# Splitting the first weight pieces of a 2:4-sparse linear layer more finely: 160, 160 and 192 columns in place of 256 and 256

## The chip, the cores and the metric

The kernel runs on one core of a Trainium2 chip. The metric is device time in microseconds (us) of one execution. Three timed executions of the kernel before gave 233.89, 233.45 and 233.73; their median is 233.73. Engines are named as in the profile: PE is TensorE (matmuls; PEld its weight loads), DVE is VectorE, ACT is ScalarE, POOL is GpSimd, and SP is the engine that here does nothing but issue DMA transfers. ACT issues transfers too.

## The reference

```python
def setup_inputs():
    B, S, D = 16, 512, 1024
    return {"x": normal(B, S, D) * 0.05, "w": normal(D, D) * 0.05, "b": normal(D) * 0.05}   # all bf16

def reference(x, w, b):
    N, M = 2, 4
    wg = w.reshape(D // M, M, D)
    mag = jnp.abs(wg)
    order = jnp.argsort(mag, 1)
    thr = jnp.take_along_axis(mag, order[:, M - N:M - N + 1, :], 1)
    mask = mag >= thr
    wp = (wg * mask).reshape(D, D)
    return jnp.einsum("bsd,df->bsf", x, wp) + b
```

In every group of four neighbouring rows of w the two entries of largest magnitude are kept in each column, and the others are set to zero. Then 8192 rows of x (64 tiles of 128) are multiplied with the 1024 x 1024 result and the bias is added.

## The kernel before, in words

The output is made in tiles of 128 rows of x by 512 columns of w (a half of the columns, h). K, 1024 long, is 8 steps of 128. A matmul of 128 x 128 weights (x) and up to 512 moving columns (w) adds into one of eight PSUM banks.

w comes in with its group of four along a free dimension (`wv`, line 60: `g p m f`, where g is the K half, m the place in the group of four). So the four candidates of a group lie side by side in one partition, and VectorE finds the mask with elementwise operations. It does this by pieces (line 61): columns 0:256, 256:512, 512:768 and 768:1024 of K half 0, then two pieces of 512 columns of K half 1. `abs_piece` (line 107, token `A.i`) makes the magnitudes, on VectorE or, for pieces 2 and 3, on ScalarE. `prep_piece` (line 122, token `P.i`) makes `hi` and `lo` (pairwise maximum and minimum), `t1`, `t2`, the threshold `thr`, the mask (line 142) and the product with w in place (line 144). For pieces 0 and 1 mask and product are made in two halves, places 0 and 1 of the group first, so that matmuls can begin with them.

The first eight tiles of x (T = 8) are treated apart, because the weights are not there yet. Their K half 0 is loaded as it lies (`load_x`, line 76), transposed on PE (`transpose_half`, line 156, token `T.t`, four 128 x 128 transposes with a stride of four), and copied from PSUM to SBUF by ScalarE (`copy_half`, line 163, token `C.t`). `mm_part` (line 170, tokens `M.i.t` and `N.i.t.m...`) multiplies tile t with piece i, for all four places m or for those named. While PE has nothing to do it runs dummy matmuls on zeros (`warm`, line 102: `W` is 512 columns, `w` 128).

Their partial sums go through `to_stage` (ScalarE, token `V`), are added to those of K half 1 (`add_stage`, `O`) and to the bias (`add_bias`, `B`). Six more tiles (`X`, `Y`) fill the time until the weights stand in natural order: `unpack` (line 149, token `U`) moves w by SBUF-to-SBUF transfers into `wp_nat`. All other x comes by transposing loads (`D`, `G`, `L`) and is multiplied in the long last loop (line 338; the last tile in `last_tile`), 50 of the 64 tiles.

The order of the instructions on every engine is written out by hand: `K` keeps the program order, the loads stand in lines 83 to 90, and all else in the string `FRONT` (line 256), which is read token by token (line 269). Each engine runs its own instructions in this order, so what is named later in `FRONT` waits behind what is named earlier on the same engine. SP's loads are one queue, ACT's two loads (line 84 and 86) another.

Of the kernel before, what the change touches and what calls it, by code (L numbers as in the profile page):

```python
# [10 lines left out]
def kernel(  # L11
# [7 lines left out]
    nc = tc.nc  # L19
    P = 128  # L20
    bf16 = mybir.dt.bfloat16
# [6 lines left out]
    B, S, D = x.shape  # L28
# [10 lines left out]
    T, F = 8, 6  # L39
# [5 lines left out]
    mags_pool = ctx.enter_context(tc.tile_pool(name="mags", bufs=3))  # L45
# [7 lines left out]
    def next_bank():  # L53
# [4 lines left out]


    wv = w.rearrange("(g p m) f -> p g m f", g=2, m=4)  # L60
    pieces = [(0, 0, 256), (0, 256, 512), (0, 512, 768), (0, 768, 1024),
              (1, 0, 512), (1, 512, 1024)]
    w_gh = {(g, h): const.tile([P, 4, FH], bf16, name=f"w_{g}_{h}") for g in range(2) for h in range(2)}

    def w_of(i):
        g, c0, c1 = pieces[i]
        return w_gh[(g, c0 // FH)][:, :, c0 % FH:c0 % FH + c1 - c0]

    def load_w(g, c0, c1, eng=nc.sync, m0=0, m1=4):
        dst = w_gh[(g, c0 // FH)][:, m0:m1, c0 % FH:c0 % FH + c1 - c0]  # L70
        K(eng.dma_start(dst, wv[:, g, m0:m1, c0:c1]))  # L71
# [4 lines left out]
    def load_x(ta, tb, eng=nc.sync):  # L76
        xt = const.tile([P, tb - ta, KH], bf16, name=f"xh_{ta}")
        src = xf[ta * P:tb * P, 0:KH].rearrange("(t p) c -> p t c", p=P)
        K(eng.dma_start(xt[:], src))  # L79
        for t in range(ta, tb):  # L80
            xh[t] = xt[:, t - ta, :]

    load_w(0, 0, 256, nc.sync, 0, 2)
    load_w(0, 0, 256, nc.scalar, 2, 4)
    load_x(0, 2)
    load_x(2, 4, nc.scalar)
    load_x(4, 6)
    load_w(0, 256, 512)
    load_x(6, 8)
    load_w(0, 512, 1024)  # L90
    bias_sb = const.tile([P, Dout], bf16, name="bias_sb")

# [9 lines left out]
    def warm(n):  # L102
        K(nc.tensor.matmul(bank[7][:, :n], lhsT=zeros[:, :P], rhs=zeros[:, :n], start=True, stop=True))  # L103
# [3 lines left out]
    def abs_piece(i, on_act):  # L107
        g, c0, c1 = pieces[i]
        n = c1 - c0
        if n <= 256:  # L110
            mag = mags_pool.tile([P, 4, n], bf16, name="mag")[:]
        else:
            mag = mag2_pool.tile([P, 4, n], bf16, name="mag2")[:]
        if on_act:
            K(nc.scalar.activation(mag, w_of(i), Act.Abs))
        else:
            for ms in (slice(0, 2), slice(2, 4)) if i == 0 else (slice(0, 4),):
                K(nc.vector.tensor_single_scalar(  # L118
                    mag[:, ms].bitcast(u16), w_of(i)[:, ms].bitcast(u16), 0x7FFF, op=Alu.bitwise_and))
        mags[i] = mag  # L120

    def prep_piece(i):
        g, c0, c1 = pieces[i]
        n = c1 - c0
        mag = mags.pop(i)
        magv = mag.rearrange("p (a j) f -> p a j f", j=2)
        hi = tmp.tile([P, 2, FH], bf16, name="hi")[:, :, :n]
        lo = tmp.tile([P, 2, FH], bf16, name="lo")[:, :, :n]
        K(nc.vector.tensor_tensor(hi, magv[:, :, 0, :], magv[:, :, 1, :], op=Alu.max))
        K(nc.vector.tensor_tensor(lo, magv[:, :, 0, :], magv[:, :, 1, :], op=Alu.min))  # L130
        t1 = tmp.tile([P, FH], bf16, name="t1")[:, :n]
        t2 = tmp.tile([P, FH], bf16, name="t2")[:, :n]
        K(nc.vector.tensor_tensor(t1, hi[:, 0, :], hi[:, 1, :], op=Alu.min))
        K(nc.vector.tensor_tensor(t2, lo[:, 0, :], lo[:, 1, :], op=Alu.max))
        thr = tmp.tile([P, FH], bf16, name="thr")[:, :n]
        K(nc.vector.tensor_tensor(thr, t1, t2, op=Alu.max))
        mask = tmp.tile([P, 4, FH], bf16, name="mask")[:, :, :n]

        halves = (slice(0, 2), slice(2, 4)) if i < 2 else (slice(0, 4),)
        for ms in halves:  # L140
            tb = thr[:, None, :].to_broadcast([P, ms.stop - ms.start, n])
            K(nc.vector.tensor_tensor(mask[:, ms], mag[:, ms], tb, op=Alu.is_ge))  # L142
        for ms in halves:
            K(nc.vector.tensor_tensor(w_of(i)[:, ms], w_of(i)[:, ms], mask[:, ms], op=Alu.mult))  # L144
# [11 lines left out]
    def transpose_half(t):  # L156
        own[(0, t)] = next_bank()
        xv = xh[t].rearrange("p (q m) -> p m q", m=4)
        dst = bank[own[(0, t)]][:].bitcast(bf16)[:, :4 * P].rearrange("p (m q) -> p m q", m=4)
        for m in range(4):  # L160
            K(nc.tensor.transpose(dst[:, m, :], xv[:, m, :], ident[:]))  # L161

    def copy_half(t):
        xt = const.tile([P, 4, P], bf16, name=f"xT_{t}")
        src = bank[own[(0, t)]][:].bitcast(bf16)[:, :4 * P].rearrange("p (m q) -> p m q", m=4)
        K(nc.scalar.copy(xt[:], src))  # L166
        xT[t] = xt


    def mm_part(q, t, c0, c1, ms=range(4)):  # L170
        g, h = divmod(q, 2)
        if c0 == 0 and (q > 0 or t >= T) and 0 in ms:
            own[(q, t)] = next_bank()
        dst = bank[own[(q, t)]][:, c0:c1]
        for m in ms:
            if t >= T:
                lhs, rhs = xN[t][:, 4 * g + m, :], wp_nat[h][:, 4 * g + m, c0:c1]
            elif g == 0:
                lhs, rhs = xT[t][:, m, :], w_gh[(0, h)][:, m, c0:c1]
            else:  # L180
                lhs, rhs = xg1[:, m, t * P:(t + 1) * P], wp_nat[h][:, 4 + m, c0:c1]
            K(nc.tensor.matmul(dst, lhsT=lhs, rhs=rhs, start=c0 == 0 and m == 0, stop=c1 == FH and m == 3))  # L182
# [54 lines left out]
    def issue_batch(t0, nb):  # L237
# [16 lines left out]


    FRONT = """
        I.1.0.512 D.0 A.0 P.0 W W W W W W W W w w T.0 T.1 C.0 T.2 T.3 C.1 w T.4 T.5 C.2 N.0.0.0 N.0.0.1 N.0.1.0
        N.0.1.1 N.0.0.2 N.0.0.3 N.0.1.2 N.0.1.3 A.1 C.3 P.1 U.0.0.0.512 I.1.512.1024 G C.4 M.0.2 C.5 M.0.3 T.6 T.7
        C.6 M.0.4 C.7 A.2 M.0.5 M.0.6 P.2 M.0.7 M.1.0 A.3 M.1.1 M.1.2 M.1.3 V.0.0 M.1.4 V.0.1 M.1.5 V.0.2 M.1.6
        V.0.3 M.1.7 V.0.4 P.3 M.2.0 V.0.5 M.2.1 V.0.6 M.2.2 V.0.7 M.2.3 M.2.4 M.2.5 M.2.6 A.4 P.4 U.1.0.0.512 D.1  # L260
        M.2.7 M.3.0 M.3.1 V.1.0 M.3.2 V.1.1 M.3.3 V.1.2 M.3.4 V.1.3 M.3.5 V.1.4 M.3.6 V.1.5 M.3.7 V.1.6 X.0.8 V.1.7
        X.0.9 V.0.8 X.0.10 V.0.9 X.0.11 V.0.10 X.0.12 V.0.11 X.0.13 V.0.12 V.0.13 A.5 P.5 U.1.1.0.512 U.0.1.0.512 Q
        L.0 L.1 N.4.0.0 N.4.1.0 N.4.2.0 N.4.3.0 N.4.0.1 N.4.1.1 N.4.2.1 N.4.3.1 N.4.0.2 N.4.1.2 N.4.2.2 N.4.3.2
        N.4.0.3 N.4.1.3 N.4.2.3 N.4.3.3 M.4.4 O.0.0 M.4.5 O.0.1 M.4.6 O.0.2 M.4.7 O.0.3 X.2.8 O.0.4 X.2.9 O.0.5
        X.2.10 O.0.6 X.2.11 O.0.7 X.2.12 O.0.8 X.2.13 O.0.9 N.5.0.0 N.5.1.0 N.5.0.1 N.5.1.1 N.5.0.2 N.5.1.2 N.5.0.3
        N.5.1.3 O.0.10 O.0.11 O.0.12 O.0.13 M.5.2 O.1.0 M.5.3 O.1.1 M.5.4 O.1.2 M.5.5 O.1.3 M.5.6 O.1.4 M.5.7 O.1.5
        O.1.6 O.1.7 Y.8 B.0.8 Y.9 B.0.9 Y.10 B.0.10 Y.11 B.0.11 Y.12 B.0.12 Y.13 B.0.13
    """
    for tok in FRONT.split():
        k, *n = tok.split(".")  # L270
        n = [int(c) for c in n]
        if k in "MN":
            g, c0, c1 = pieces[n[0]]
            h = c0 // FH
            mm_part(2 * g + h, n[1], c0 - h * FH, c1 - h * FH, n[2:] or range(4))
        elif k in "Ww":
            warm(FH if k == "W" else P)
        elif k == "A":
            abs_piece(n[0], 2 <= n[0] < 4)
        elif k == "P":  # L280
            prep_piece(n[0])
        elif k == "T":
            transpose_half(n[0])
        elif k == "C":
            copy_half(n[0])
        elif k == "Z":
            mm_part(n[0], n[1], 0, FH, n[2:])
        elif k == "I":
            load_w(*n)
        elif k == "D":  # L290
            load_fill(*n)
        elif k == "G":
            K(nc.sync.dma_start_transpose(out=xg1[:], in_=xf[0:T * P, KH:D]))
        elif k == "Q":
            for f in (slice(0, FH), slice(FH, Dout)):
                K(nc.sync.dma_start(bias_sb[:, f], b[f].partition_broadcast(P)))
        elif k == "X":
            mm_part(n[0], n[1], 0, FH)
        elif k == "V":
            to_stage(*n)  # L300
        elif k == "O":
            add_stage(*n)
        elif k == "B":
            add_bias(*n)
        elif k == "U":
            unpack(*n)
        elif k == "Y":
            bk = next_bank()
            mm_nat(n[0], 1, bk)
            evac_dve(n[0], 1, bk)  # L310
        elif k == "L":
            issue_batch(*batches[n[0]])
# [60 lines left out]
```

## Time and profile before

| | us |
|---|---|
| timed, median of 3 (233.45 to 233.89) | 233.73 |
| profiled execution: span from first to last instruction | 231.5 |
| timed median less the span | 2.2 |
| PE busy in the span | 226.3 (98%) |
| DVE busy | 119.9 (52%) |
| ACT busy | 18.8 (8%) |

The page gives the profiled execution's span and no other time of it; the timed median is of other executions of the same program, and what lies around the span is their difference.

PE's busy share over the 40 slices of the span:

```profile
PE   7999999999999999999999999999999999999995
DVE  4899887867987424424424423423433433433433
ACT  3977500000000000000000000000000000000000
```

Each digit is a slice of 5.8 us, in tenths. PE is full from the second slice on; DVE is nearly full in the first ten and half idle later; ACT works in the first five slices only. Matmul records show starts exactly and ends by a model, so rates are read from start to start. A few records are missing.

### The profile page before, as it was taken

The page shows a single profiled execution, that of the slowest core. Times are in us where ns is not written, and L with a number is a line of the kernel's source. Part 1 is how long each engine was busy: PE and PEld are TensorE (multiplying, and loading weights), DVE is VectorE, ACT ScalarE, POOL GpSimd, SP SyncE. Part 2 cuts the span into 40 slices and gives each one's busy share as a digit, 9 for nine tenths or more (in the row PEclk, how much of TensorE's full clock was granted, in tenths as well). Part 3 has the DMA queues.
Part 4 walks back from the last instruction along what each step waited for, and adds up shares of the span by engine and source line. Part 5 has one row for each costly group of instructions (what it writes and reads, how often), then busy time and mean ns, then how long its engine had stood idle before and what let it go on. Part 6 is the DMA issues. An engine that isn't in the chain of part 4 may idle for free.

```text
span 231.5 us, 2724 instructions
## 1 busy us (share of the span) xinstructions
PE 226.3 (98%) x1128; PEld 110.6 (48%) x1147; DVE 119.9 (52%) x204; ACT 18.8 (8%) x34; POOL 0.7 (0%) x6
## 2 busy tenths in 40 slices
PE   7999999999999999999999999999999999999995
PEld 3887444444444444444444444444444444444443
DVE  4899887867987424424424423423433433433433
ACT  3977500000000000000000000000000000000000
POOL 1000000000000000000000000000000000000000
DMA  6999889999847221995239822696129991122222
GB/s 194 319 200 242 190 178 178 253 246 296 295 181 272 91 83 34 239 201 172 93 75 238 230 93 91 120 258 197 63 91 197 188 249 46 47 91 91 91 93 91
DMA packets 76972, 38.19 MB, mean 165 GB/s; under 512 B 62752, under 2 KB 68896, under 8 KB 76960
## 3 DMA queue, kind: packets, MB, share of 16 engines
q1 hardware_dynamic: 67696, 20.91, 45.2%
q10 hardware_dynamic: 9264, 17.11, 20.4%
q8 instruction: 9, 0.15, 0.3%
q14 instruction: 3, 0.02, 0.0%
HBM read 3.41 MB, written 16.78 MB: 87 GB/s over the span
## 4 chain that ended last, share of the span: by engine, by line
PE 96%; DMA 2%; issue 1%; SPq 0%; DVE 0%
PE bank L338 73%; PE bank L182 16%; PE bank L234 6%; DMA xh<-in_x_dram 2%; PE bank L161 0%; SPq L79 0%; SPq L71 0%; DVE o_last L323 0%
## 5 line engine op out<-in xcount | busy, mean ns | idle before, releaser
L338 PE MATMUL bank<-wp_nat,xTb 128*128 128x512 bf16 x737 | 161.7, 379 | 0.8
L219 DVE TENSOR_TENSOR o_pair<-bank,bias_sb 128x512 bf16<-128x512 f32 x104 | 67.3, 686 | 99.6 <-PE bank L338 94.2
L338 PEld LDWEIGHTS <-xTb 128*128 128x128 bf16 x752 | 73.6, 98 | 88.7
L210 DVE TENSOR_TENSOR stage<-bank,stage 128x512 f32<-128x512 f32 x22 | 14.4, 686 | 3.9 <-PE bank L182 3.8
L182 PE MATMUL bank<-w,xT 128*128 128x256 bf16 x128 | 14.3, 273 | 0.0
L214 DVE TENSOR_TENSOR o_pair<-stage,bias_sb 128x512 bf16<-128x512 f32 x22 | 14.0, 682 | 0.0
L182 PE MATMUL bank<-wp_nat,xg 128*128 128x512 bf16 x62 | 13.9, 379 | 0.1
L182 PEld LDWEIGHTS <-xT 128*128 128x128 bf16 x128 | 12.5, 98 | 1.4
L206 ACT COPY stage<-bank 128x512 f32<-128x512 f32 x22 | 11.4, 618 | 3.9 <-PE bank L182 3.9
L182 PE MATMUL bank<-wp_nat,xfill 128*128 128x512 bf16 x47 | 10.6, 379 | 0.1
L234 PE MATMUL bank<-wp_nat,xfill 128*128 128x512 bf16 x47 | 10.5, 379 | 0.1
L182 PEld LDWEIGHTS <-xg 128*128 128x128 bf16 x64 | 6.3, 98 | 7.6
L234 PEld LDWEIGHTS <-xfill 128*128 128x128 bf16 x48 | 4.7, 98 | 5.7
L182 PEld LDWEIGHTS <-xfill 128*128 128x128 bf16 x48 | 4.7, 98 | 5.5
L338 PE MATMUL bank<-wp_nat,xTs 128*128 128x512 bf16 x32 | 7.1, 379 | 0.0
L142 DVE TENSOR_TENSOR mask<-mag,thr 128x512 bf16<-128x512 bf16 (+2 forms) x8 | 5.4, 690 | 0.2
L144 DVE TENSOR_TENSOR w<-w,mask 128x512 bf16<-128x512 bf16 (+2 forms) x8 | 5.3, 688 | 0.1
L103 PE MATMUL bank<-zeros 128*128 128x512 bf16 (+1 forms) x11 | 4.0, 533 | 1.2 <-DVE zeros L96 1.2
L338 PEld LDWEIGHTS <-xTs 128*128 128x128 bf16 x32 | 3.1, 98 | 3.8
L166 ACT COPY xT<-bank 128x512 bf16<-128x512 bf16 x8 | 4.1, 607 | 2.7 <-PE bank L161 2.7
L118 DVE TENSOR_SCALAR mag<-w 128x512 uint16<-128x512 uint16 (+2 forms) x5 | 2.3, 477 | 2.7 <-DMA w<-in_w_dram 2.7
L234 PE MATMUL bank<-wp_nat,xTb 128*128 128x128 bf16 (+2 forms) x32 | 3.7, 272 | 0.0
(20 smaller groups left out, 26.9 us busy)
## 6 DMA issues: line engine op xcount, KB each, us to landing
out_dram<-o_pair ACTq DMA_DIRECT2D x31, 512.0 KB, 2.8
wp_nat<-w SPq DMA_DIRECT2D x16, 128.0 KB, 2.8
w<-in_w_dram SPq DMA_DIRECT2D x3, 512.0 KB, 6.0
xh<-in_x_dram SPq DMA_DIRECT2D x3, 256.0 KB, 4.5
xh<-in_x_dram ACTq DMA_DIRECT2D x1, 256.0 KB, 4.0
w<-in_w_dram SPq DMA_DIRECT2D x1, 256.0 KB, 5.1
bias_sb<-in_b_dram SPq DMA_DIRECT2D x2, 128.0 KB, 3.7
out_dram<-o_pair ACTq DMA_DIRECT2D x1, 256.0 KB, 2.0
```

What stands on the lines that cost most here:

```text
L103: K(nc.tensor.matmul(bank[7][:, :n], lhsT=zeros[:, :P], rhs=zeros[:, :n], start=True, stop=True))
L118: K(nc.vector.tensor_single_scalar(mag[:, ms].bitcast(u16), w_of(i)[:, ms].bitcast(u16), 0x7FFF, op=Alu.bitwise_and))
L142: K(nc.vector.tensor_tensor(mask[:, ms], mag[:, ms], tb, op=Alu.is_ge))
L144: K(nc.vector.tensor_tensor(w_of(i)[:, ms], w_of(i)[:, ms], mask[:, ms], op=Alu.mult))
L166: K(nc.scalar.copy(xt[:], src))
L182: K(nc.tensor.matmul(dst, lhsT=lhs, rhs=rhs, start=c0 == 0 and m == 0, stop=c1 == FH and m == 3))
L206: K(nc.scalar.copy(stage[(h, t)][:], bank[own[(h, t)]][:]))
L210: K(nc.vector.tensor_tensor(st, bank[own[(2 + h, t)]][:], st, op=Alu.add))
L214: K(nc.vector.tensor_tensor(get_o(t)[:, f], stage.pop((h, t))[:], bias_sb[:, f], op=Alu.add))
L219: K(nc.vector.tensor_tensor(get_o(t)[:, f], bank[bk][:], bias_sb[:, f], op=Alu.add))
L234: K(nc.tensor.matmul(bank[bk][:, :c1 - c0], lhsT=xN[t][:, kt, :], rhs=wp_nat[h][:, kt, c0:c1], start=kt == 0, stop=kt == KT - 1))
L338: K(nc.tensor.matmul(bank[bks[h]][:], lhsT=xN[t][:, kt, :], rhs=wp_nat[h][:, kt, :], start=kt == 0, stop=kt == KT - 1))
```

## The change

The two pieces of 256 columns become three of 160, 160 and 192. The first load brings columns 0:320 (half by SP, half by ACT), and the later one 320:512. The first x load, of two tiles by SP, becomes two of one tile each, one by SP and one by ACT; tiles 2 and 3 move from ACT to SP, tiles 4 and 5 from SP to ACT; and tiles 6 and 7 go ahead of the second weight load. The magnitudes of piece 1 are made by ScalarE and of pieces 0 and 2 by VectorE. The first three pieces have mask and product in halves. `FRONT` is rewritten: four `w` dummies in place of two before T.0, transposes and matmuls of the first pieces interleaved otherwise. All later pieces have a number one higher, with the same order among them.

```diff
-    pieces = [(0, 0, 256), (0, 256, 512), (0, 512, 768), (0, 768, 1024),
+    pieces = [(0, 0, 160), (0, 160, 320), (0, 320, 512), (0, 512, 768), (0, 768, 1024),
               (1, 0, 512), (1, 512, 1024)]
...
-    load_w(0, 0, 256, nc.sync, 0, 2)
-    load_w(0, 0, 256, nc.scalar, 2, 4)
-    load_x(0, 2)
-    load_x(2, 4, nc.scalar)
-    load_x(4, 6)
-    load_w(0, 256, 512)
+    load_w(0, 0, 320, nc.sync, 0, 2)
+    load_w(0, 0, 320, nc.scalar, 2, 4)
+    load_x(0, 1)
+    load_x(1, 2, nc.scalar)
+    load_x(2, 4)
+    load_x(4, 6, nc.scalar)
     load_x(6, 8)
+    load_w(0, 320, 512)
     load_w(0, 512, 1024)
...
-            mag = mags_pool.tile([P, 4, n], bf16, name="mag")[:]
+            mag = mags_pool.tile([P, 4, 256], bf16, name="mag")[:, :, :n]
...
-        halves = (slice(0, 2), slice(2, 4)) if i < 2 else (slice(0, 4),)
+        halves = (slice(0, 2), slice(2, 4)) if i < 3 else (slice(0, 4),)
...
-        I.1.0.512 D.0 A.0 P.0 W W W W W W W W w w T.0 T.1 C.0 T.2 T.3 C.1 w T.4 T.5 C.2 N.0.0.0 N.0.0.1 N.0.1.0
-        N.0.1.1 N.0.0.2 N.0.0.3 N.0.1.2 N.0.1.3 A.1 C.3 P.1 U.0.0.0.512 I.1.512.1024 G C.4 M.0.2 C.5 M.0.3 T.6 T.7
-        C.6 M.0.4 C.7 A.2 M.0.5 M.0.6 P.2 M.0.7 M.1.0 A.3 M.1.1 M.1.2 M.1.3 V.0.0 M.1.4 V.0.1 M.1.5 V.0.2 M.1.6
...
+        I.1.0.512 D.0 A.0 A.1 P.0 W W W W W W W W w w w w T.0 T.1 C.0 T.2 T.3 w C.1 N.0.0.0.1 C.2 P.1
+        N.0.0.2.3 T.4 N.0.1.0.1 C.3 T.5 N.0.2.0.1 N.0.1.2.3 C.4 T.6 N.0.3.0.1 N.0.2.2.3 C.5 T.7 N.0.4.0.1
+        N.0.3.2.3 C.6 N.0.4.2.3 A.2 M.0.5 N.1.0.0.1 C.7 P.2 U.0.0.0.512 I.1.512.1024 G N.1.0.2.3 M.0.6
+        N.1.1.0.1 N.0.7.0.1 A.3 N.0.7.2.3 N.1.1.2.3 M.1.2 M.1.3 N.1.4.0.1 A.4 N.1.4.2.3 M.1.5 M.1.6 P.3
+        M.1.7 M.2.0 M.2.1 V.0.0 M.2.2 N.2.3.0.1 V.0.1 N.2.3.2.3 M.2.4 V.0.2 M.2.5 N.2.6.0.1 V.0.3 N.2.6.2.3
...
-            abs_piece(n[0], 2 <= n[0] < 4)
+            abs_piece(n[0], n[0] in (1, 3, 4))
```

More of the change, by code (lines that the diff above doesn't have):

```diff
@@ L256 @@
     FRONT = """
-        I.1.0.512 D.0 A.0 P.0 W W W W W W W W w w T.0 T.1 C.0 T.2 T.3 C.1 w T.4 T.5 C.2 N.0.0.0 N.0.0.1 N.0.1.0
-        N.0.1.1 N.0.0.2 N.0.0.3 N.0.1.2 N.0.1.3 A.1 C.3 P.1 U.0.0.0.512 I.1.512.1024 G C.4 M.0.2 C.5 M.0.3 T.6 T.7
-        C.6 M.0.4 C.7 A.2 M.0.5 M.0.6 P.2 M.0.7 M.1.0 A.3 M.1.1 M.1.2 M.1.3 V.0.0 M.1.4 V.0.1 M.1.5 V.0.2 M.1.6
-        V.0.3 M.1.7 V.0.4 P.3 M.2.0 V.0.5 M.2.1 V.0.6 M.2.2 V.0.7 M.2.3 M.2.4 M.2.5 M.2.6 A.4 P.4 U.1.0.0.512 D.1
-        M.2.7 M.3.0 M.3.1 V.1.0 M.3.2 V.1.1 M.3.3 V.1.2 M.3.4 V.1.3 M.3.5 V.1.4 M.3.6 V.1.5 M.3.7 V.1.6 X.0.8 V.1.7
@@ L262 @@
[L262 to L266, printed above, removed]
@@ L267 @@
-        O.1.6 O.1.7 Y.8 B.0.8 Y.9 B.0.9 Y.10 B.0.10 Y.11 B.0.11 Y.12 B.0.12 Y.13 B.0.13
+        I.1.0.512 D.0 A.0 A.1 P.0 W W W W W W W w w w w T.0 T.1 C.0 T.2 T.3 w C.1 N.0.0.0.1 C.2 P.1
+        N.0.0.2.3 T.4 N.0.1.0.1 C.3 T.5 N.0.2.0.1 N.0.1.2.3 C.4 T.6 N.0.3.0.1 N.0.2.2.3 C.5 T.7 N.0.4.0.1
+        N.0.3.2.3 C.6 N.0.4.2.3 A.2 M.0.5 N.1.0.0.1 C.7 P.2 U.0.0.0.512 I.1.512.1024 G N.1.0.2.3 M.0.6
+        N.1.1.0.1 N.0.7.0.1 A.3 N.0.7.2.3 N.1.1.2.3 M.1.2 M.1.3 N.1.4.0.1 A.4 N.1.4.2.3 M.1.5 M.1.6 P.3
@@ new lines @@
+        M.1.7 M.2.0 M.2.1 V.0.0 M.2.2 N.2.3.0.1 V.0.1 N.2.3.2.3 M.2.4 V.0.2 M.2.5 N.2.6.0.1 V.0.3 N.2.6.2.3
+        N.2.7.0.1 V.0.4 N.2.7.2.3 P.4 M.3.0 V.0.5 M.3.1 V.0.6 M.3.2 V.0.7 M.3.3 M.3.4 M.3.5 M.3.6 A.5 P.5
+        U.1.0.0.512 D.1 M.3.7 M.4.0 M.4.1 V.1.0 M.4.2 V.1.1 M.4.3 V.1.2 M.4.4 V.1.3 M.4.5 V.1.4 M.4.6 V.1.5
+        M.4.7 V.1.6 X.0.8 V.1.7 X.0.9 V.0.8 X.0.10 V.0.9 X.0.11 V.0.10 X.0.12 V.0.11 X.0.13 V.0.12 V.0.13
+        A.6 P.6 U.1.1.0.512 U.0.1.0.512 Q L.0 L.1 N.5.0.0 N.5.1.0 N.5.2.0 N.5.3.0 N.5.0.1 N.5.1.1 N.5.2.1
@@ L268 @@
+        N.5.3.1 N.5.0.2 N.5.1.2 N.5.2.2 N.5.3.2 N.5.0.3 N.5.1.3 N.5.2.3 N.5.3.3 M.5.4 O.0.0 M.5.5 O.0.1
+        M.5.6 O.0.2 M.5.7 O.0.3 X.2.8 O.0.4 X.2.9 O.0.5 X.2.10 O.0.6 X.2.11 O.0.7 X.2.12 O.0.8 X.2.13 O.0.9
+        N.6.0.0 N.6.1.0 N.6.0.1 N.6.1.1 N.6.0.2 N.6.1.2 N.6.0.3 N.6.1.3 O.0.10 O.0.11 O.0.12 O.0.13 M.6.2
+        O.1.0 M.6.3 O.1.1 M.6.4 O.1.2 M.6.5 O.1.3 M.6.6 O.1.4 M.6.7 O.1.5 O.1.6 O.1.7 Y.8 B.0.8 Y.9 B.0.9
+        Y.10 B.0.10 Y.11 B.0.11 Y.12 B.0.12 Y.13 B.0.13
     """
```

## The prediction

> **What bounds the kernel now.** I read the page first (busy shares, chain by engine), then the chain in order of time, then the timelines of TensorE (PE), VectorE (DVE) and ScalarE (ACT) up to 30 us, then the DMA issues. The page's chain by engine, and the first steps of the chain in time (start, length, what):
>
> ```profile
> PE 96%; DMA 2%; issue 1%; SPq 0%; DVE 0%
> ```
>
> ```profile
> 1.74 4.53 DMA xh<-in_x_dram
> 6.28 0.05 issue
> 6.32 0.64 PE bank L161 x8
> 6.96 1.79 PE bank L182 x16
> 8.75 0.45 PE bank L161 x8
> 9.19 13.31 PE bank L182 x117
> ```
>
> The chain is PE from 6.32 us to the last tile; ahead of it stands one load of x, tiles 4 and 5 (landed 1.74 + 4.53 = 6.27). The PE timeline (start, length, line, operation) shows how little idle there is:
>
> ```profile
> 1.19 3.81 PE L103 MATMUL bank<-zeros 128*128 128x512 bf16 x10 [1.19 <-DVE zeros L96]
> 4.96 1.17 PE L161 MATMUL bank<-ident,xh 128*128 128x128 bf16 x16
> 5.96 0.22 PE L103 MATMUL bank<-zeros 128*128 128x128 bf16 x1
> 6.32 0.64 PE L161 MATMUL bank<-ident,xh 128*128 128x128 bf16 x8
> 6.84 1.91 PE L182 MATMUL bank<-w,xT 128*128 128x256 bf16 x16
> 8.58 0.61 PE L161 MATMUL bank<-ident,xh 128*128 128x128 bf16 x8
> 9.03 12.39 PE L182 MATMUL bank<-w,xT 128*128 128x256 bf16 x112
> 21.25 5.34 PE L182 MATMUL bank<-wp_nat,xfill 128*128 128x512 bf16 x23
> 26.43 6.86 PE L182 MATMUL bank<-wp_nat,xg 128*128 128x512 bf16 x31
> ```
>
> Starts are what count, since ends are modelled. 8.58 to 9.03 is 8 transposes, 56 ns each; 9.03 to 21.25 is 112 matmuls of 256 columns, 109 ns; 21.25 to 26.43 is 24 of 512 columns (one record missing), 216 ns. From 6.32 on nothing waits. From T.0 (4.96) to the first 512-column matmul (21.25) is 16.29 us; the work in it is 32 x 0.056 + 128 x 0.109 + one dummy 0.056 = 15.8. So the front, which is all that the change touches, holds 0.5 us that could go: about 0.1 is the first transposes, and 0.3 is the wait before 6.32. That is 0.2% of the run.
>
> VectorE and ScalarE make what PE consumes there:
>
> ```profile
> 3.61 0.52 DVE L118 TENSOR_SCALAR mag<-w 128x512 uint16<-128x512 uint16 x2 [2.48 <-DMA w<-in_w_dram]
> 4.16 0.43 DVE L129 TENSOR_TENSOR hi<-mag 128x512 bf16<-128x512 bf16 x1
> 6.37 0.75 DVE L144 TENSOR_TENSOR w<-w,mask 128x512 bf16<-128x512 bf16 x2
> 7.34 0.43 DVE L118 TENSOR_SCALAR mag<-w 128x1024 uint16<-128x1024 uint16 x1 [0.22 <-DMA w<-in_w_dram]
> 11.07 0.43 DVE L129 TENSOR_TENSOR hi<-mag 128x512 bf16<-128x512 bf16 x1 [0.31 <-ACT mag L115]
> 16.78 0.68 DVE L118 TENSOR_SCALAR mag<-w 128x2048 uint16<-128x2048 uint16 x1
> ```
>
> ```profile
> 5.49 3.03 ACT L166 COPY xT<-bank 128x512 bf16<-128x512 bf16 x6 [2.21 <-PE bank L161]
> 9.96 2.02 ACT L115 ACTIVATE mag<-w 128x1024 bf16<-128x1024 bf16 x2
> ```
>
> Piece 0 takes VectorE 3.5 us (3.61 to 7.12); its first half is ready at 6.37 + 0.42 = 6.79 and PE's first real matmul starts at 6.84. ScalarE copies transposed tiles 0.48 us apart.
>
> **The change, part by part.** The sum goes against the profiled execution: span 231.5; the timed median is 233.73, so 2.2 us lie around the span and are taken as unchanged.
>
> *Loads.* From issue to landing, the DMA rows give: w halves 0.73 + 2.9 = 3.6 (SP) and 0.73 + 3.1 = 3.8 (ACT), x0-1 1.24 + 3.7 = 4.9, x2-3 1.25 + 4.0 = 5.3, w 256:512 2.25 + 5.1 = 7.3, x6-7 8.1, w 512:1024 9.6. From 3.0 to 4.4 us 374 GB/s moved, 0.18 us per 64 KB. The first w pair grows by 64 KB, so it lands at 3.75 and 4.0. x0 and x1 end after 576 KB where 512 KB (w, x0-1) stood before: 4.6 to 5.0. x2-3 was the end of 768 KB at 5.3; if its turn still comes before x4-5 it ends 832 KB, 5.5; if it shares equally with x4-5, which now goes by ACT's queue, both end 1088 KB, 5.3 + 320 KB at 374 GB/s = 6.2. The queue order between them decides; these are the two ends, and I take 5.6, nearer the first, because x2-3 of before landed only 0.4 after x0-1. x6-7 then ends near 6.9 and w 320:512 near 7.4. ACT's third issue (0.5 us) puts its table load from 1.79-3.07 to 2.3-3.6, hidden: its first work, A.1, waits for w until 4.0. One wait is new: the program has eight DMA semaphores in rotation, and with one load more w 512:1024 is the ninth, so SP holds it until the first w half lands (about 3.8; before, w of the second K half stood there). Behind it on SP stand only that load and the first transposing load, and the engines are busy with earlier loads until 7.4 in any case, so it costs nothing.
>
> *Warm-up.* Two more dummies of 128 columns at the slow clock: the two of before stand at 4.57 and 4.68, 0.107 apart, so they now end at 5.0 instead of 4.79; T.0 waited for x until 4.96, so it moves by 0.04. T.0 and T.1 end at 5.56.
>
> *VectorE.* No row has 160 or 192 columns. Tensor-tensor: 256 elements last 0.285 (next start after 0.202), 512 0.42 (0.34), 1024 0.69 (0.61): a straight line, so 160: 0.235 (0.15), 320: 0.32 (0.24), 192: 0.25 (0.17), 384: 0.35 (0.27). Ends: the 256 price for all (no gain at all), or proportional; I take the line, since three rows lie on it. A.0 with the second half at 4.0 ends at 4.27. P.0: hi 4.30, lo 4.54, t1 4.78, t2 4.93, thr 5.20, masks 5.47 and 5.71, products 5.95 and 6.19: halves ready at 6.27 and 6.51 (6.79 and 7.12 before). P.1: its magnitudes come from ScalarE, 0.72 us (0.9 ns an element, between the 512-element copy at 0.61 and the 1024-element abs at 1.06) from 4.0, done 4.7, ahead of C.0 (5.55), so nobody waits. hi at 6.43, halves ready at 8.40 and 8.64. A.2 on VectorE at 8.56 (0.36; w landed about 7.4, 1.1 us in hand), halves 11.13 and 11.40. P.3 starts at 11.32 (A.3 follows C.7, done by 10.7), ready at 14.25; P.4 17.11; A.5 at 17.04 against 16.78, 0.26 later.
>
> *PE.* 160 columns: between 56 ns (128) and 109 (256), 216 for 512 also on the line: 69; 192: 82.5. Ends: the 128 and the 256 price; I take the line. 512 columns of eight tiles: 64 x 0.069 + 32 x 0.0825 = 7.07 against 64 x 0.109 = 6.99, so +0.08. T.2, T.3 follow T.1 at 5.65 and end with the dummy at 6.18; N.0.0 waits for VectorE's half, 6.27 + 0.05 = 6.32, and its second half until 6.56, a wait of 0.1. Then T.4 to T.7 (0.9) stand between. Copies C.2 to C.7, 0.48 apart from 5.55, finish at 7.1, 7.6, 8.05, 8.5, 9.0, 9.5; PE reaches their users at 7.3, 7.8, 8.3, 8.7, 9.3, 9.7. Piece 1 is wanted at 9.0, piece 2 at 11.8 (ready 11.4), piece 3 at 14.4 (14.25), piece 4 at 17.9 (17.1). The tightest covers are 0.15 us, on VectorE at piece 3 and on the copies; what slips beyond goes one to one into the end. First 512-column matmul: 6.32 + 0.1 + 0.9 + 7.07 + 64 x 0.109 = 21.4 against 21.25: **+0.1 us**.
>
> *Later.* U.0 waits for P.2 (11.4) but SP issues the first transposing load until 11.6 anyway. U.1.0 (SP, waits for P.5, 22.47) goes to 22.7; it lands 2.5 later, wanted at 26.43: over 1 us in hand. Behind it on SP, D.1 (25.0 + 6.9 = 31.9, wanted 33.34) has 1.4. V.0.0 starts after A.4 (about 11.5) when M.2.0 ends (12.1), and its banks are free by 16.4 against 17.5 wanted. From 21.4 on the stream is the same.
>
> Sum: 231.5 + 0.1, median 233.73 + 0.1 = 233.85: no difference that can be told (0.2%, 0.47 us, is about what a measurement of this kernel can tell). The 0.3 us wait for x4-5 goes, since T.4 now stands behind the first real matmuls; what is late next is VectorE's first half.
>
> The loaded piece of 192 columns has runs of 384 bytes. The Trainium skill (DMA: Bandwidth & Descriptors, Specifications) has runs below 512 bytes miss the line rate. At half the rate of the rows, an estimate, w 320:512 would land at 8.0 instead of 7.4, still before 8.56, so by the rule the sum stands and only its cover shrinks; no row here has 384 bytes.
>
> **The rivals.**
> 1. *x2-3 comes late (slower).* The transfer of x4-5 ran in a stretch (4.4 to 5.6) of only 268 GB/s. If x2-3 shares its turn with x4-5 at that rate, 320 KB take 1.2 us: it lands at 6.5, N.0.0 starts at 7.1, and the end moves by 0.75: 234.5. It decides from a landing at 6.2. For: two queues now carry 256 KB each at once. Against: SP's x2-3 is issued with less ahead of it. At the full rate (6.2) the cost is 0.45, 234.2, at the edge of the bound.
> 2. *The slow clock lasts longer (slower).* Transposes went from 107 to 56 ns apart at about 5.2, 4 us after the first dummy. A pause of PE near 5.6 to 6.3 could hold a rise that has not come yet: at half rate from 6.3 to 8.6 it costs 1.1: 234.9. Against: before also paused (6.02 to 6.32) after the rise. The Trainium skill (TensorE: Matmul & The Clock Gate, Part 1) has a free-running window of 3.4 us decide; the trace agrees with the 4 us, not with more.
> 3. *Small pieces cost VectorE what 256 columns cost (slower).* Then piece 2 is ready 2 us later, 235.8. The three rows on a line speak against it.
> 4. *Matmuls of 160 and 192 columns at the 128 price (faster).* 64 x 13 + 32 x 27 ns = 1.7 less: 232.0, if VectorE kept up, which with 0.15 us of cover it would not; so at best some 0.3, 233.4. The same floor holds if w lands no later than before: N.0.0 at 6.2, 233.6.
>
> **How the numbers follow.** The forecast with its own range 233.5 to 234.2: 0.70. Rival 1: 0.13; rival 2: 0.04; rival 3 or another stall of over half a microsecond in the front: 0.04. Rival 4 or a front better than the 0.5 us of idle allows, and a measurement that drifts: 0.09. Faster 0.09, same 0.70, slower 0.21. The range takes in the floor (233.4) and rival 1 (234.5), leaving out 0.15.
>
> **What would show it.** T.0 at 5.0; x2-3's transposes at 5.6 without idle; first 160-column matmul at 6.3, 69 ns apart; VectorE's A.2 near 8.6; no PE idle at pieces 2 and 3; first 512-column matmul at 21.4. Wrong if PE idles over 0.3 us before the first x2-3 transposes, or before M.2 or M.3.

## The result and the profile after

The changed kernel took 236.53 us (median of six executions, 234.94 to 237.14) beside 233.53 for the kernel before (six, 233.30 to 233.89). The ratio is 1.0121, with a 95% interval of 1.0099 to 1.0144. It is slower by 3.0 us. The forecast was 233.85, no difference, with a range up to 234.5.

In the profiled execution of the changed kernel (237.14 us, span 235.3) PE's timeline over the front reads (start, length, line, operation, then the idle time ahead of it and what ended it):

```profile
4.57 0.98 PE L162 MATMUL bank<-ident,xh 128*128 128x128 bf16 x8
7.88 0.64 PE L162 MATMUL bank<-ident,xh 128*128 128x128 bf16 x8 [2.33 <-DMA xh<-in_x_dram]
8.41 0.44 PE L183 MATMUL bank<-w,xT 128*128 128x160 bf16 x4
9.75 0.74 PE L183 MATMUL bank<-w,xT 128*128 128x160 bf16 x4
11.67 13.49 PE L183 MATMUL bank<-w,xT 128*128 128x160 bf16 x146
25.00 5.34 PE L183 MATMUL bank<-wp_nat,xfill 128*128 128x512 bf16 x23
```

T.0 and T.1 start at 4.57, and then PE stands for over two microseconds until the load of tiles 2 and 3 has landed. The first 512-column matmul starts at 25.00 where it started at 21.25 before. From there to the last matmuls the two traces run alike: the last tile's matmuls begin at 228.91 against 225.16, and 3.75 us is also the difference at 25.00. So all of the loss is made in the front.

The load that PE waits for, by the DMA issues of the two kernels (SP's load issued at 1.74 in both; last number: us from issue to landing). Before, it was tiles 4 and 5:

```profile
xh<-in_x_dram SPq DMA_DIRECT2D x1, 256.0 KB, 4.5
```

In the changed kernel it is tiles 2 and 3:

```profile
xh<-in_x_dram SPq DMA_DIRECT2D x1, 256.0 KB, 6.1
```

It landed at 1.74 + 6.1 = 7.84. The trace has 16 completion events for such a load, one for each part of it. 15 of them came by 6.04, and the last one 1.8 us later. Each of the three loads that followed (x4-5 on ACT's queue, x6-7 and w 320:512 on SP's) has one such late part too, 0.9 to 1.4 us behind the fifteenth. One packet of 1 KB, begun at 5.08, took 0.97 us; in the two traces of the kernel before (the second is c0 below) no packet between 2 and 8 us took over 0.45. That fits one share of the transfers that fell behind on both queues; which one, and why, the trace doesn't tell.

A second loss stands in the stages of the changed kernel (stretch, its length, busy us and instructions of each engine, granted clock, DMA share, GB/s):

```profile
5.50:8.70 3.20, 0.86 (x15) 0.82 (x15) 2.66 (x12) 1.18 (x3) 0.00 (x0) 1.00 0.95 274
8.75:12.15 3.40, 3.40 (x32) 3.40 (x30) 2.75 (x10) 2.55 (x6) 0.00 (x0) 0.50 1.18 264
12.20:25.00 12.80, 12.80 (x145) 12.08 (x144) 11.16 (x23) 9.08 (x17) 0.00 (x0) 1.00 1.02 209
```

In a stretch of 3.2 us PE was busy for 0.86 us; for the 3.4 us that followed its granted clock was 0.50. In the timeline above, four matmuls of 160 columns span 0.44 us at 8.41 and 0.74 at 9.75. The Trainium skill (TensorE: Matmul & The Clock Gate, Part 1) tells of a free-running window of about 3.4 us at whose end PE's activity in it decides the clock. The trace agrees: the half rate lasts from 8.74 to 12.15, one such length, and follows a stretch in which PE was mostly idle. One such stretch makes a mean granted clock of 0.993 over the whole span, and three of the six executions have that mean (236.57 to 237.14). Two more, at 236.45 and 236.50, have 1.000; no trace shows what made them slow.

### The profile page after: what moved, and what is told of

The parts are those of the page before. It is cut to its first block, busy times and chain, and to the rows that moved or that the text cites. A ratio compares the mean times of both kernels' runs of the same rounds, so it can differ in the third digit from the quotient of the medians.

```text
span 235.3 us, 2805 instructions
## 1 busy us (share of the span) xinstructions
PE 227.9 (97%) x1161; PEld 113.5 (48%) x1180; DVE 120.6 (51%) x213; ACT 19.9 (8%) x35; POOL 0.7 (0%) x6
## 3 DMA queue, kind: packets, MB, share of 16 engines
HBM read 3.41 MB, written 16.78 MB: 86 GB/s over the span
## 4 chain that ended last, share of the span: by engine, by line
PE 95%; DMA 3%; issue 1%; SPq 0%; DVE 0%
PE bank L342 72%; PE bank L183 17%; PE bank L235 6%; DMA xh<-in_x_dram 3%; PE bank L162 1%; SPq L79 0%; SPq L71 0%; DVE o_last L327 0%; PE bank L104 0%
## 5 line engine op out<-in xcount | busy, mean ns | idle before, releaser
L183 PE MATMUL bank<-w,xT 128*128 128x160 bf16 (+2 forms) x160 | 15.9, 260 | 0.0
L183 PEld LDWEIGHTS <-xT 128*128 128x128 bf16 x160 | 14.2, 103 | 0.7
L162 PE MATMUL bank<-ident,xh 128*128 128x128 bf16 x32 | 4.1, 285 | 2.3 <-DMA xh<-in_x_dram 2.3
L143 DVE TENSOR_TENSOR mask<-mag,thr 128x320 bf16<-128x320 bf16 (+3 forms) x10 | 5.6, 582 | 0.2
L145 DVE TENSOR_TENSOR w<-w,mask 128x320 bf16<-128x320 bf16 (+3 forms) x10 | 5.6, 580 | 0.1
L162 PEld LDWEIGHTS <-xh 128*128 128x128 bf16 x32 | 3.3, 140 | 2.5 <-DMA xh<-in_x_dram 2.5
```

## The experiments

The times below are medians; every ratio is to runs of the kernel before on the same chip.

**a1 to a4: the loads, or the pieces?**

a1 is the changed kernel once more.

> The changed kernel itself once more, unchanged. In its first trace PE stood idle from 5.5 to 7.9 us in front of T.2 (waiting for x2-3, whose 16 parts had landed by 6.04 except one at 7.84), and from 8.7 to 12.1 its matmuls ran at half rate (160 columns every 133 ns instead of 69). Theory A (the loads: x2-3 now shares with x4-5 and lands late; the idle that follows lets the clock drop): the idle is there again, at least 0.5 us, and wherever it is over 1 us the half rate follows; time 235 to 237. Rival B (the late part was an accident of one execution; pieces and order cost the rest): landing near 6.0, idle 0.5, no half rate in the trace, time still 236.

It took 234.65 (ten executions, 233.93 to 236.72; ratio 1.0054, interval 1.0030 to 1.0078). That is below the expected 235 to 237, and the interval doesn't overlap with that of the first six executions (1.0099 to 1.0144). In its trace (235.89 us) the gap is there again, T.2 starting at 6.95:

```profile
6.95 1.04 PE L162 MATMUL bank<-ident,xh 128*128 128x128 bf16 x8 [1.17 <-DMA xh<-in_x_dram]
10.67 12.05 PE L183 MATMUL bank<-w,xT 128*128 128x160 bf16 x135
```

Here the clock did not drop; it rose late. The matmuls of 160 columns came 133 ns apart until 9.8 us, and 69 after. The page's granted clock reads 1.00 in that slow stretch too, as it does over the dummies at the start, so a mean of 1.000 doesn't rule out slow matmuls in the front. The load landed late in both traces of this kernel, by different amounts, and its times vary.

a2 puts the x loads back.

```diff
-    load_x(0, 1)
-    load_x(1, 2, nc.scalar)
-    load_x(2, 4)
-    load_x(4, 6, nc.scalar)
+    load_x(0, 2)
+    load_x(2, 4, nc.scalar)
+    load_x(4, 6)
     load_x(6, 8)
```

> The changed kernel with the x loads of before: tiles 0-1 by SP, 2-3 by ACT, 4-5 by SP, 6-7 ahead of the second w load as in the change. Theory A: x2-3 lands near 5.5, T.2 follows T.1 without idle, N.0.0 starts at 6.2 to 6.5, no half rate; 233.3 to 234.0. Rival B (pieces, order, ScalarE's magnitudes): it stays at 236 or more.

It took 233.62 (ten, 233.34 to 234.00; 1.0007, interval 0.9997 to 1.0017): no difference from the kernel before. Its PE timeline:

```profile
5.13 1.08 PE L161 MATMUL bank<-ident,xh 128*128 128x128 bf16 x16 [0.35 <-DMA xh<-in_x_dram]
6.22 0.45 PE L182 MATMUL bank<-w,xT 128*128 128x160 bf16 x4
21.36 1.24 PE L182 MATMUL bank<-wp_nat,xfill 128*128 128x512 bf16 x5
```

All 16 transposes of T.0 to T.3 run without a gap, the first real matmul starts at 6.22, and the first 512-column matmul at 21.36. Everything in the change but the x loads costs and gains nothing that these runs can tell. Rival B fell.

This run also splits the loss of the profiled execution. N.0.0 started at 8.41 in the changed kernel and at 6.22 here: 2.19 us of waiting. From N.0.0 to the first 512-column matmul took 16.59 us against 15.14: 1.45 us more, under the half clock. Together 3.64, and 25.00 - 21.36 = 3.64. (3.41 us at half rate lose 1.7 us. By an estimate from the distances of its matmuls, a2 has some 0.2 us of small waits in the same part, which explains most of the difference.)

a3 is the other direction: the kernel before, with the x loads of the change alone (and tiles 6-7 ahead of w 256:512).

```diff
-    load_x(0, 2)
-    load_x(2, 4, nc.scalar)
-    load_x(4, 6)
-    load_w(0, 256, 512)
+    load_x(0, 1)
+    load_x(1, 2, nc.scalar)
+    load_x(2, 4)
+    load_x(4, 6, nc.scalar)
     load_x(6, 8)
+    load_w(0, 256, 512)
```

> The kernel before with the x loads of the change alone: tiles 0 and 1 singly, 2-3 by SP, 4-5 by ACT, 6-7 ahead of the second w load. Pieces, order and magnitudes as before. Theory A: T.2 to T.5 wait, N.0.0 starts at 7 or later, and if the idle is long the half rate follows: 234.3 to 237. Rival B: 233.4 to 233.8, as before.

It took 235.56 (ten; 1.0086, interval 1.0055 to 1.0117). The ten fall into two groups of five: 234.10 to 234.86, and 236.26 to 236.92. In four of the upper five the mean granted clock was 0.993, in all of the lower five 1.000. The profiled execution (234.61) is one of the lower five. The x loads alone make the loss.

a4 fills the gap with dummies.

```diff
-        ... T.0 T.1 C.0 T.2 T.3 w C.1 N.0.0.0.1 C.2 P.1
+        ... T.0 T.1 C.0 W W W W W W T.2 T.3 w C.1 N.0.0.0.1 C.2 P.1
```

> The changed kernel with six dummy matmuls of 512 columns between T.1 and T.2, so that PE is busy for some 1.3 us (at full rate) of the idle stretch. They remove no wait and, where x2-3 lands before 6.9, add one. Theory A with the clock as its larger part: the half rate between 8.7 and 12.1 goes and with it some 1.7 us: 234.3 to 235.2. If the half rate has nothing to do with PE's idle time: 236.5 or more.

It took 234.88 (four, 234.23 to 234.92; 1.0053, interval 1.0036 to 1.0069), without a half rate in its trace. But a1, without dummies, was at 234.65 on the same chip and had only one execution at a lower mean clock; so this run alone doesn't show what the clock costs. That was taken up again in f1.

**b1 to b3: which of the loads?**

> The changed kernel with one load moved back: x4-5 goes by SP instead of ACT. Tiles 0 and 1 stay single, x2-3 stays on SP. Theory A1 (x2-3 is late because x4-5 shares the transfer engines with it from the other queue): x2-3 lands by 5.7, x4-5 near 6.4, no long idle before T.2, 233.4 to 234.0. Theory A2 (it is late because transfers of one tile each, 8 pieces per engine and a completion, lower the rate: 3.4 to 4.6 us moved 250 to 340 GB/s in the changed kernel against 340 to 390 before): the rate between 3.4 and 4.6 stays under 320, x2-3 lands after 6, 234 or more.

```diff
-    load_x(4, 6, nc.scalar)
+    load_x(4, 6)
```

The changed kernel with that took 234.16 (four, 233.84 to 234.44; 1.0016, interval 0.9989 to 1.0043, not told apart from the kernel before). x2-3 landed at 5.9 and PE waited 0.32 us. The rates were 355 and 314 GB/s in 3.4 to 4.6, and 193 in the 0.6 us after it. That speaks for neither theory in full. The landing is earlier than in the traces with x4-5 on ACT's queue (6.5 to 7.8), so the sharing of the two queues may matter; but the interval overlaps with a1's, and a dip is there with x4-5 behind x2-3, too.

> The kernel before with one edit: tiles 0 and 1 singly, 0 by SP and 1 by ACT. x2-3 by ACT and x4-5 by SP as before. Theory A1: hardly a change, 233.3 to 233.8 (x2-3 and x4-5 already overlap in the same way as before). Theory A2: the rate between 3.4 and 4.6 falls under 320 GB/s, T.4 starts after 6.6 instead of 6.32, 234 or more.

```diff
-    load_x(0, 2)
+    load_x(0, 1)
+    load_x(1, 2, nc.scalar)
     load_x(2, 4, nc.scalar)
```

This one edit in the kernel before took 235.56 (four, 234.49 to 236.72; 1.0077, interval 1.0027 to 1.0127). Theory A1 fell: the split alone, with x2-3 and x4-5 on their old queues, does it. x2-3 landed at 7.7, and PE waited 2.69 us for it (2.33 in the changed kernel):

```profile
7.71 1.05 PE L162 MATMUL bank<-ident,xh 128*128 128x128 bf16 x8 [2.69 <-DMA xh<-in_x_dram]
```

The two stretches in its trace:

```profile
3.40:4.00 0.60, 0.60 (x3) 0.20 (x2) 0.39 (x2) 0.36 (x2) 0.00 (x0) 1.00 0.81 231
4.00:4.60 0.60, 0.60 (x8) 0.40 (x7) 0.57 (x3) 0.00 (x0) 0.00 (x0) 1.00 0.42 116
```

and the same of the kernel before:

```profile
3.40:4.00 0.60, 0.60 (x3) 0.19 (x2) 0.39 (x2) 0.00 (x0) 0.00 (x0) 1.00 1.08 386
4.00:4.60 0.60, 0.60 (x3) 0.17 (x2) 0.57 (x3) 0.00 (x0) 0.00 (x0) 1.00 1.04 342
```

The last number is what the transfers moved, 116 GB/s in place of 342.

> The kernel before with one edit: x2-3 goes by SP and x4-5 by ACT, tiles 0 and 1 stay a pair. Since T.2 to T.5 stand ahead of the first real matmul, and x2-3 is now behind x0-1 on SP, x2-3 should land where x4-5 did, 6.3, and N.0.0 start at 7.2 instead of 6.84: 234.0 from the order alone. Theory A1: x2-3 lands at 6.8 or later, PE idles over 1 us, 234.5 to 237 with the slow clock in some runs. Theory A2: rates as before (over 340 GB/s in 3.4 to 4.6), landing 6.2 to 6.5, 233.8 to 234.3.

```diff
-    load_x(2, 4, nc.scalar)
-    load_x(4, 6)
+    load_x(2, 4)
+    load_x(4, 6, nc.scalar)
```

It took 234.69 (four, 234.41 to 234.88; 1.0038, interval 1.0011 to 1.0065). The figures of theory A1 came (x2-3 at 6.9, PE idle 1.48 us, the time), those of A2 did not. But neither gives the reason. There is no small transfer, yet 3.4 to 4.6 moved 90 and 167 GB/s, and x0-1, the first x load, whose place in its queue had not changed, landed at 5.7 instead of 4.9. What differs up to that point is which load ACT's queue moves beside it: the rows of tiles 4-5 instead of 2-3, into another tile of SBUF.

**c0 to e2: the rows in DRAM**

c0 is a second trace of the kernel before.

> The kernel before once more, for a second trace of its first loads. If the transfer rate of the first loads belongs to the pattern of loads, 3.4 to 4.6 us moves 340 GB/s or more again, as in its first trace (386, 342), and T.4 starts at 6.2 to 6.6. If dips such as those of the runs with other loads (90 to 290 GB/s there) come by chance, one may be here.

The rates were 369 and 381, T.4 started at 6.34, the time 233.32. The good rate belongs to that pattern of loads.

In c1 queues, order, sizes and destinations are those of the kernel before, and only the source rows of two loads are exchanged. `load_x` gets a fourth argument for it, the tile whose rows it reads.

```diff
-    def load_x(ta, tb, eng=nc.sync):
+    def load_x(ta, tb, eng=nc.sync, frm=None):
...
-        src = xf[ta * P:tb * P, 0:KH].rearrange("(t p) c -> p t c", p=P)
+        f0 = ta if frm is None else frm
+        src = xf[f0 * P:(f0 + tb - ta) * P, 0:KH].rearrange("(t p) c -> p t c", p=P)
...
-    load_x(2, 4, nc.scalar)
-    load_x(4, 6)
+    load_x(2, 4, nc.scalar, 4)
+    load_x(4, 6, nc.sync, 2)
```

> The kernel before with the rows in DRAM of two loads exchanged: the ACT load for tiles 2 and 3 reads the rows of tiles 4 and 5, and the SP load for 4 and 5 those of 2 and 3 (so the first K half of these four tiles is multiplied for the wrong rows). Queues, sizes, order, destinations and all later work stay as before. Theory A3 (what slows the first loads is which DRAM rows are read at the same time: tiles 0-1 with 4-5 lie 1 MB apart, with 2-3 half a MB): a dip under 250 GB/s in 3.4 to 4.6 as in the run with the queues exchanged (90, 167), x0-1 lands after 5.3, 234 or more. Otherwise the time stays at 233.3 to 233.8 and the dip comes from queue, destination or the small transfers.

It took 234.41 (eight, 234.15 to 236.21; 1.0054, interval 1.0027 to 1.0081), and its stretches are:

```profile
3.40:4.00 0.60, 0.60 (x3) 0.19 (x2) 0.56 (x3) 0.00 (x0) 0.00 (x0) 1.00 0.93 121
4.00:4.60 0.60, 0.60 (x3) 0.17 (x2) 0.60 (x3) 0.00 (x0) 0.00 (x0) 1.00 0.78 200
```

x0-1 landed at 6.1 instead of 4.9. With all else equal, the rows that are read at the same time changed the rate.

c2 is the split with both single tiles on SP.

```diff
-    load_x(0, 2)
+    load_x(0, 1)
+    load_x(1, 2)
```

> The kernel before with tiles 0 and 1 loaded singly, both by SP one after the other; 2-3 by ACT and 4-5 by SP as before. So there is one small transfer more, but the two queues read the same rows at the same time as before. Theory A2 (small transfers lower the rate): under 320 GB/s in 3.4 to 4.6, 234 or more, as with one tile on each queue (235.6). Theory A3 (what the two queues read at the same time): rate as before, T.4 at 6.2 to 6.6, 233.3 to 233.9.

It took 234.26 (ten, 233.38 to 236.12; 1.0042, interval 1.0015 to 1.0069). 3.4 to 4.0 moved 358 GB/s, 4.0 to 4.6 only 212; half of tile 1's parts had landed at 5.0, the last at 6.4. A split within one queue costs, too. Whether it costs less than one over two queues, the overlapping intervals of c2 and b2 don't tell. The two queues read the same rows as before here, so the rows don't explain this dip.

d1 and d2 move the rows in other ways (again by the fourth argument).

```diff
 # d1
-    load_x(0, 2)
-    load_x(2, 4, nc.scalar)
-    load_x(4, 6)
+    load_x(0, 2, nc.sync, 4)
+    load_x(2, 4, nc.scalar, 6)
+    load_x(4, 6, nc.sync, 0)
...
-    load_x(6, 8)
+    load_x(6, 8, nc.sync, 2)
```

> The kernel before, rows in DRAM exchanged so that the relation of what is read at the same time is kept and the place is not: the load of tiles 0-1 reads the rows of 4-5, that of 2-3 (ACT) those of 6-7, that of 4-5 the rows of 0-1, that of 6-7 the rows of 2-3 (so the first K half of tiles 0 to 7 is multiplied for the wrong rows). Theory A3 (the relation counts: two pairs half a MB apart are fast, as in the kernel before): 340 GB/s or more in 3.4 to 4.6, T.0 at 5.0, 233.3 to 233.9. Rival A5 (the place counts: the rows of tiles 4-5 are slow when they are first read, wherever they stand): under 250 in 3.4 to 4.6, x0-1 lands after 5.3, 234 or more.

233.37 (ten; 0.9991, interval 0.9978 to 1.0004), 345 and 309 GB/s. The rows of tiles 4-5 are not slow in themselves: rival A5 fell.

```diff
 # d2
-    load_x(2, 4, nc.scalar)
+    load_x(2, 4, nc.scalar, 6)
...
-    load_x(6, 8)
+    load_x(6, 8, nc.sync, 2)
```

> The kernel before, with the ACT load of tiles 2-3 reading the rows of 6-7 and the load of 6-7 those of 2-3 (wrong rows for these four tiles in the first K half): the two loads that run together now lie 1.5 MB apart instead of half a MB; tiles 0-1 and 4-5 as before. Theory A3 in its plain form (only neighbours half a MB apart are fast): a dip under 250 in 3.4 to 4.6, 234 or more. If distance counts only as a power of two (1 MB slow, 1.5 MB not), or if the place counts and only 4-5 is slow (A5): rate as before, 233.3 to 233.9.

233.53 (ten; 1.0001, interval 0.9990 to 1.0012), 374 and 311 GB/s. 1.5 MB apart is as good as half a MB, so the plain form of A3 fell, and its form by the distance stayed.

```diff
 # e1
-    load_x(2, 4, nc.scalar)
+    load_x(2, 4, nc.scalar, 8)
```

> The kernel before, with the ACT load of tiles 2-3 reading the rows of tiles 8-9, 2 MB from those of 0-1 that SP reads at the same time (wrong rows for two tiles in the first K half). If whole MB apart is what is slow: a dip under 250 GB/s in 3.4 to 4.6 as at 1 MB (121, 200), 234 or more. If 1 MB alone is: rate as before (340 or more), 233.3 to 233.9.

235.60 (ten, 234.45 to 237.18; 1.0077, interval 1.0049 to 1.0105), but not in the way that either side expected:

```profile
3.40:4.00 0.60, 0.60 (x3) 0.20 (x2) 0.38 (x2) 0.00 (x0) 0.00 (x0) 1.00 1.08 386
4.60:5.20 0.60, 0.07 (x2) 0.00 (x0) 0.60 (x3) 0.00 (x0) 0.00 (x0) 1.00 1.00 162
5.20:5.80 0.60, 0.14 (x3) 0.14 (x3) 0.53 (x3) 0.00 (x0) 0.00 (x0) 1.00 0.55 138
```

In 3.4 to 4.0, while SP read tiles 0-1 and ACT 8-9, 2 MB apart, the rate was full; in 4.0 to 4.6 it was 263. It fell further when SP came to tiles 4-5 (from 4.55, by the order of its packets) while ACT was still on 8-9 (to 5.7): those lie 1 MB apart. So three traces (b3, c1, e1) show the dip where two x loads 1 MB apart run together. Of the traces without a split none shows it in 3.4 to 4.0 at 0.5, 1.5 or 2 MB.

The changed kernel hardly has this case: by the order of its packets SP has read tile 0 by 3.9, and ACT begins tiles 4-5 at 4.3. The x loads that it runs together lie 0.5 MB apart or less. So this distance is not what made its loss.

e2 asks whether the split is slow for the same reason.

```diff
-    load_x(0, 2)
-    load_x(2, 4, nc.scalar)
-    load_x(4, 6)
+    load_x(0, 1)
+    load_x(1, 2, nc.scalar, 3)
+    load_x(2, 4, nc.scalar, 7)
+    load_x(4, 6, nc.sync, 5)
```

> The kernel before with tiles 0 and 1 loaded singly, one by SP and one by ACT, which took 235.6, and with other rows in DRAM: the ACT single reads tile 3, the SP pair that follows reads 5 and 6, the ACT pair 7 and 8 (so the first K half of five tiles is multiplied for the wrong rows). No two loads that run together then lie whole MB apart. Theory A2 (small transfers are slow as such): under 250 in 3.4 to 4.6 as with the true rows (231, 116), 235 or more. Theory A3 (rows read together): 300 or more in 3.4 to 4.6, 233.4 to 234.2.

Most of the rate came back, 285 and 314 GB/s against 231 and 116 in b2. The time did not: 235.64 (ten; 1.0077, interval 1.0042 to 1.0111).

```profile
7.23 0.90 PE L163 MATMUL bank<-ident,xh 128*128 128x128 bf16 x8 [2.19 <-DMA xh<-in_x_dram]
```

PE waited for ACT's pair: half of its parts had landed at 5.8, the last one at 7.2. SP's pair was alike, 5.6 and 7.0. So the low rate and the late last part are two things: the rows go far to explain the first in b2, and what makes single parts of a load lag by 1.4 us stays open.

**f1: the clock**

```diff
 # in a3
-        ... T.0 T.1 C.0 T.2 T.3 C.1 w T.4
+        ... T.0 T.1 C.0 W W W W W W T.2 T.3 C.1 w T.4
```

> The kernel before with the x loads of the change (as in a3) and six dummies of 512 columns between T.1 and T.2. They can't bring x2-3 earlier. If the upper group of a3 (236.3 to 236.9, five of ten) is the half clock after PE's idle time, it is gone: all executions within 234.1 to 235.3, no half rate in the trace. If it is x2-3 landing later in those executions, they stay at 236 to 237.

234.92 (four, 234.82 to 235.30; 1.0057, interval 1.0040 to 1.0074). Its trace shows a late load, and the clock up:

```profile
7.44 0.64 PE L162 MATMUL bank<-ident,xh 128*128 128x128 bf16 x8 [0.38 <-DMA xh<-in_x_dram]
```

```profile
8.75:12.15 3.40, 3.40 (x39) 3.11 (x37) 2.88 (x9) 2.45 (x6) 0.00 (x0) 1.00 1.20 270
```

x2-3 landed at 7.4, later than in a3's trace (7.0), and still no execution came near a3's upper group of 236.3 to 236.9. If half of the executions belonged to that group whatever the dummies do, four of four would stay out of it once in sixteen by luck; a4's four stayed out as well. So the dummies most likely hold the clock, and the distance between a3's groups, some 2 us, is then mostly the half clock; no execution of the upper group was traced.

## Why the prediction was wrong

*The loads: wrong, and this is the step that failed.* The forecast worked out the landing of x2-3 as the bytes ahead of it over one rate, 374 GB/s, measured mostly while x0-1 and x2-3 ran together as pairs. From it came 5.6 us for x2-3 with 5.5 and 6.2 as both ends. Measured were 7.84 (the changed kernel), 6.9 (a1) and 6.5 (a4). In the changed kernel the rate was not the main miss: 15 of the 16 parts of x2-3 had landed by 6.04, between the two ends. The last part came at 7.84, and the sum had no term for a part that lags. Such a lag is no row of the trace of before, where the last part of an x load came at most 0.6 us after its median part. The x loads make the loss (a2, a3), and the split of the first of them is enough for it (b2: x2-3 at 7.7); why a part lags stays open. The rate, too, belongs to the loads that run together and not to the queues (c1: 386 to 121 GB/s by exchanged rows alone). So the bound from above was no bound: it let the bytes ahead vary, kept the rate, and took all parts to land together. The prediction's own sign of being wrong, PE idle for over 0.3 us before the transposes of x2-3, came with 2.33 us.

*Rival 1, late x2-3:* the right place, with too small a price. It used 268 GB/s, shared with x4-5, for its end of 6.5 us and 234.5; all three landings were at or past it. The sharing is not the reason by itself: in b2 x2-3 and x4-5 stand on their old queues, and x2-3 landed at 7.7.

*Rival 2, the clock:* given 0.04 and 1.1 us. It cost 1.45 in the profiled execution. A rise that is held back, as the rival had it, is what a1's trace shows; in the profiled execution the clock had risen and fell again. The error was to set the two rivals beside each other as alternatives. With the loads in time (a2) there is no half rate: the clock is slow because the load is late, so their prices add, 2.2 + 1.45. The range's upper end, rival 1 alone, left out the very case that came. How far the median lies beyond that end varies: 2.0 us in the first six executions, 0.15 in a1's ten.

*The warm-up:* miscounted. The forecast took the dummies to end at 5.0, with two of 128 columns more. It overlooked that `FRONT` now has seven `W` in place of eight, 0.43 us less at the slow clock. (The diff in the section on the change prints eight `W` in the new line; the kernel has seven.) T.0 started at 4.57 (tile 0 landed at 4.4), and PE went idle that much earlier, which lengthened the gap without changing its end.

*VectorE, ScalarE and matmuls: right.* 320 elements lasted 0.32 and 160 0.23 us (forecast 0.32, 0.235), the abs of 640 elements 0.73 (0.72), matmuls of 160 and 192 columns came 69 and 82 to 83 ns apart (69, 82.5). In a2, where the loads are those of before, the first real matmul started at 6.22 (6.32) and the first 512-column matmul at 21.36, where the forecast had 21.4. The sum of +0.1 us is what a2 shows: 1.0007, within noise.

*The first w pair:* forecast 3.75 and 4.0, landed 3.4 and 3.6 in the changed kernel, 3.6 and 3.8 in a2; 64 KB more didn't delay it measurably (3.6 and 3.8 before).

*Runs of 384 bytes:* half the rate, the forecast's own estimate for them, did not come. In a2 the stretch 6.4 to 7.0, in which 380 of the 451 packets are such runs of w 320:512, shows 337 GB/s:

```profile
6.40:7.00 0.60, 0.60 (x12) 0.57 (x11) 0.60 (x4) 0.60 (x2) 0.00 (x0) 1.00 1.15 337
```

The stretches of 0.6 us ahead of it and behind it, mostly runs of 1 KB, moved 374 and 380, and the load landed at 7.8. The Trainium skill (DMA: Bandwidth & Descriptors, Specifications) has runs below 512 bytes miss the line rate. The traces here don't settle it: the runs of 512 bytes of the kernel before were no faster (330 in 5.8 to 6.4), and in a4, where the loads ahead were late, 250 and 183 GB/s were moved in 6.4 to 7.0 and 7.0 to 7.6, mostly by runs of 384. In the changed kernel it landed at 9.2, behind the late loads and with a late part of its own, and VectorE waited 0.99 us for it; PE was later still.

*Everything after the front:* no stall of PE was added, as forecast.

## What to carry to other kernels

A transfer rate read from a trace belongs to the loads that were in flight together, their shapes and their addresses. When a change regroups the first loads, a landing worked out from the best stretch is no bound: leave room for a lower rate and for a single late part, of which the trace of before need not show any. Where PE waits at the start of a kernel, add the clock to the price of the wait: in the profiled execution 2.2 us of waiting cost 3.6. If a gap can't be avoided, dummies in it may hold the clock (f1, a4: eight executions, none beyond 235.3).

## What the hardware showed that was not expected

Two loads of 256 KB whose rows lie 1 MB apart, in flight on two queues, moved 90 to 200 GB/s together (b3, c1; 138 to 162 in e1). Pairs 0.5 or 1.5 MB apart moved 309 to 386 in the same stretch (before, c0, d1, d2), and 2 MB apart 386 (e1, 3.4 to 4.0). The Trainium skill (DMA: Bandwidth & Descriptors, Latency and other measured facts) tells of something akin, a lower rate where the rows of a tile are large powers of two apart, and calls channel aliasing an inference. The runs here show a distance between two loads, with 1 MB slow and 2 MB not, and don't show the mechanism either.

In the runs with single tiles the last of the 16 parts of x2-3 (in c2 of x4-5) landed 0.8 to 2.3 us after the median part; for the x pairs of the two traces of the kernel before it is 0.2 to 0.6. With other rows the rate was better and the lag stayed (e2). Without a split, c1, d1 and e1 show lags of 0.9 to 1.0; d1's median time (0.9991) shows no loss by it. What makes it was not found.

The half rate went with PE's busy time. Four traces have it: the changed kernel, b2, e1 and e2. In each it began 3.41 us after the clock had risen and lasted 3.41 us. In the 3.41 us ahead of it PE was busy for 1.07, 1.01, 1.64 and 1.22 us. In c2, b3, a3 and f1, in the 3.41 us that followed the rise of the clock, PE was busy for 1.80, 1.93, 2.06 and 2.91 us, and no half rate came. So in these traces the line lies between 1.64 and 1.80 us, about a half of the stretch, and c2's gap of 1.6 us was short enough. No run was made to test that.
